# h of batches 6 and 7 in 512-token pieces, their loads in halves, and a new order behind the first operations

## The chip, the cores and the metric

One core of one Trainium2 chip runs the whole program. The metric is the device time of one execution in microseconds (us), the median over runs. The core has five engines that work side by side and wait for each other by semaphores: TensorE (PE in the profile; PEld is its weight load), VectorE (DVE), ScalarE (ACT), GpSimd (POOL) and SyncE (SP). The last two mostly issue DMAs here.

## The reference

Linear attention with a norm, and then a gated feed-forward block, for 8 batches of 576 tokens. The inputs are float32.

```python
kv = einsum('bhsd,bhse->bhde', k, v)          # 8 heads of 64
o = einsum('bhsd,bhde->bhse', q, kv)
o = o / sqrt(mean(o * o, -1) + 1e-6) * g_norm
x = o with heads side by side                  # 576 x 512 for a batch
h = relu(x @ w_in)                             # 576 x 1024
c[s] = w0 * h[s-1] + w1 * h[s] + w2 * h[s+1]   # conv_w, each channel by itself
out = (h * sigmoid(c)) @ w_out                 # 576 x 512
```

## The kernel before, in words

Everything on chip is bfloat16 except sums in PSUM and the rows that go out. The batches are handled in pairs (0,1), (2,3), (4,5), (6,7); h of a pair is one tile of 128 channels x 8 blocks x 1152 tokens. PSUM is cut into 8 banks by hand.

The program is a list of small operations, each a few instructions. A string, `ORDER` (lines 71 to 135), names them in the order in which they are written into the program, and lines 671 to 679 tie the instructions of each engine to exactly this order. Each engine takes its instructions one after the other; between engines only the data, the PSUM banks and the buffers make them wait. A token is a name with arguments, `!A` or `!V` for ACT or DVE where either could do it, and behind `@` the bank or buffer that its tile gets. The operations, with their lines:

- `Lq`, `Lk`, `Lv` (352 to 363): POOL issues the load of q, k or v of a batch. With a second argument 0 or 1 it is half a batch (288 KB as bfloat16), without it the whole (576 KB). q, k and v have two buffers each, so a load waits until the batch that had the buffer has been read. A load also waits for the load eight before it.
- `kv` (386): PE sums k'v of a batch, 72 matmuls of 64x64, or 36 for a half. `kvc` copies it to SBUF.
- `qt` (411) and `qc` (422): PE transposes q by halves, 36 matmuls each; ACT or DVE copies it.
- `ot` (432): PE makes o, 8 matmuls for half a batch. `sq` (446) squares it on ACT, `oc` (451) keeps it.
- `ss` (477), `ln` (489), `sl` (495): the sums of squares of a pair, the reciprocal root on ACT, and on DVE its split into two bfloat16 parts. `sp` (505) spreads it over the channels on PE and `mu` (516) multiplies on DVE, which makes x. A pair's `ss` needs all eight `sq` of its two batches.
- h in either of two ways. `hm` (529) works on one batch: two halves of 288 tokens, so 128x288 matmuls, with two of the four parts of x in one step; `re` (539) is its relu. `ha` (543) works on a pair, flat over its 1152 tokens: 512 of them at a time, four matmuls; `hb` (556) does the last 128 tokens for four channel blocks, 16 matmuls of 128x128. Their relus are `rea` and `reb`. Batches 0, 1, 6 and 7 go by `hm`, pairs (2,3) and (4,5) by `ha` and `hb`.
- the gate: `ta` (580) two taps, `aa` (587) and `ab` (593) their sums, on DVE; `sg` (599) the sigmoid on ACT; `mg` (606) the product with h on DVE, in place.
- `om` (614): PE multiplies h by w_out, four of the eight channel blocks in one step of four 128x512 matmuls, into one bank; `ea` (633) copies the finished bank into a row buffer (four of them), `st` (641) stores it from SP. Blocks 0 and 1, 2 and 3, and so on of a pair share a store.
- `sw` (660): the next store is held back until the named load has landed.
- `fi`, `fq`, `fo`: matmuls of zeros that fill time on PE.

Of the lists at the top, `CONV`, `OMT`, `NORM`, `HALFOUT` and `STORES2` are read by the program; `STORES2` only says which stores go out as two of 256 KB instead of one of 512 (line 648). `HALF` and `PAIRH` are read nowhere: what they name stands in the order.

The core of `ha` and `hm`:

```python
for t in (2 * u, 2 * u + 1):          # hm: b, f, u
    for e in range(2):
        nc.tensor.matmul(ps[:, e, :HS], w_in_sb[:, t, f * P:(f + 1) * P], x[:, t, e * HS:(e + 1) * HS], ...)
...
for t in range(NT):                   # ha: p, f, e
    nc.tensor.matmul(ps, w_in_sb[:, t, f * P:(f + 1) * P], x[:, t, e * 512:(e + 1) * 512], ...)
```

Of the kernel before, what the change touches and what calls it, by code (L numbers as in the profile page):

```python
# [68 lines left out]


# [20 lines left out]
qc.3.0!V@0 oc.3.3@2 aa.1.0 mg.1.3 sq.3.3@4 om.0.1.1.0@2 oc.3.2 ta.1.3@1 om.0.1.0.0 ea.0.1.0!A@1 Lk.5.1@0 Lq.4.1@1
ta.1.2 om.0.1.0.1@6 om.0.0.1.0 ab.1.0 sq.3.2@5 ea.0.0.0!A aa.1.1 ab.1.1 om.0.1.1.1 sg.1.0 qt.5.1@0 qt.5.0@2 kv.3.0@4
qc.5.1!V@1 sg.1.1 ea.0.1.1!V qc.5.0!V@2 kvc.3.0!A Lq.4.0 om.0.2.1.1@7 mg.1.0 sg.1.3 sg.1.2 ot.3.0@0,4 om.0.2.1.0@6
sq.3.1@6 om.0.3.1.1@2 Lv.5.1@0 sq.3.0@7 ss.2@3 ss.3 ln.1@0 mg.1.1 oc.3.1@3 oc.3.0 sl.1@0 om.0.2.0.1 om.0.3.0.1 st.0.0
ea.0.3.1!A@2 kv.5.1@4 qt.4.1@0 Lk.5.0 sp.3.1.1@2 kvc.5.1!V Lk.4.1@1 mu.3.1.1@0 sp.2.0.1@4 mu.2.0.1 om.0.2.0.0
qc.4.1!A@0 sp.3.0.0@0 sp.3.1.0@2 ea.0.2.1!A@0 om.0.3.1.0@7 sp.3.0.1@4 mu.3.0.0 Lv.5.0 sp.2.1.1@0 mu.3.1.0 om.0.3.0.0
mu.3.0.1 sp.2.1.0@2 ea.0.2.0!A sp.2.0.0@4 mu.2.1.1 mu.2.0.0 mu.2.1.0 hb.1.0@6 Lv.4.1@1 fq.1.256.0@0 kv.4.1@0
ea.0.3.0!A kv.5.0@4 reb.1.0!A@1 kvc.5.0!V ot.5.1@6,2 kvc.4.1!A sq.5.2@0 oc.5.2@0 sq.5.3@1 ha.1.3.0@0 rea.1.3.0!V
ha.1.3.1@1 rea.1.3.1!V oc.5.3 ta.2.3@0 Lk.4.0 ot.5.0@6,4 ha.1.2.0@0 Lv.4.0 rea.1.2.0!V ha.1.2.1@3 oc.5.0@1 rea.1.2.1!V
ta.2.2 sq.5.1@2 Lk.7@0 oc.5.1 aa.2.1 ha.1.1.1@1 kv.4.0@4 sq.5.0@3 rea.1.1.1!A ot.4.1@6,2 kvc.4.0!A qt.4.0@0 oc.4.2@2  # L100
sq.4.3@4 qc.4.0!V@0 ab.2.1 oc.4.3 sq.4.2@5 ha.1.1.0@4 rea.1.1.0!A ta.2.1@1 ha.1.0.0@5 rea.1.0.0!A ha.1.0.1@2
ot.4.0@0,3 rea.1.0.1!A ta.2.0 aa.2.0 sq.4.1@6 sq.4.0@7 ha.1.6.0@5 ha.1.5.1@2 ss.4@6 oc.4.1@3 oc.4.0 ss.5 rea.1.5.1!A
ln.2@0 Lq.7@0 qt.7.1@3 qc.7.1!A@0 qt.7.0@0 om.0.4.0@2 sl.2@0 om.0.4.1 ab.2.0 ha.1.5.0@3 Lv.7@0 rea.1.6.0!A sp.5.0.1@4
sp.5.1.1@6 mu.5.0.1@1 qc.7.0!A@1 Lv.6@1 ea.0.4!A@3 sp.4.1.1@0 mu.4.1.1 ha.1.4.0@2 rea.1.5.0!A sg.2.0 hb.1.1@3 Lq.6@1
mu.5.1.1 sp.5.1.0@0 rea.1.4.0!V sp.5.0.0@4 kv.7@6 ha.1.4.1@2 reb.1.1!A kvc.7!A sp.4.0.0@6 mu.5.0.0 mu.5.1.0 sg.2.1
rea.1.4.1!A sp.4.1.0@4 mu.4.0.0 sp.4.0.1@0 mu.4.1.0 ha.1.7.1@3 sg.2.3 mu.4.0.1 sw.q.6 st.0.4 hb.2.1@2 reb.2.1!V@0
sg.2.2 ot.7.0@4,6 mg.2.0 Lk.6@1 ta.2.5@1 rea.1.7.1!A oc.7.1@0 ta.2.4 kv.6@0 ha.1.7.0@2 kvc.6!V sq.7.1@0 ha.2.3.0@3
oc.7.0 ha.2.7.0@6 sq.7.0@1 aa.2.2 ha.1.6.1@7 rea.1.7.0!A ot.7.1@4,0 rea.2.3.0!A rea.1.6.1!V ab.2.2 rea.2.7.0!A
qt.6.0@2 ha.2.7.1@6 oc.7.2@1 sq.7.3@2 sq.7.2@3 oc.7.3 ha.2.6.0@7 mg.2.1 ta.2.6@0 sg.2.4 qc.6.0!V@0 rea.2.7.1!A
ha.2.2.0@4 ha.2.1.0@0 ha.2.4.0@1 rea.2.4.0!V ha.2.3.1@5 sg.2.5 ta.2.7 rea.2.6.0!A rea.2.1.0!A rea.2.2.0!A aa.2.3  # L110
sw.k.6 st.0.3 ab.2.3 rea.2.3.1!A mg.2.2 ha.2.0.0@2 qt.6.1@0 rea.2.0.0!A ot.6.0@6,3 ta.3.7@1 oc.6.0@2 sq.6.0@4
ha.2.6.1@5 oc.6.1 ha.2.5.1@2 ha.2.2.1@6 qc.6.1!A@0 rea.2.6.1!A sw.k.6 st.0.2 sq.6.1@5 sg.2.6 ta.3.6 ha.2.1.1@7 aa.3.3
sg.2.7 mg.2.3 rea.2.1.1!A hb.2.0@0 om.1.2.0.1@1 ha.2.0.1@3 ab.3.3 reb.2.0!A rea.2.2.1!A rea.2.0.1!A om.1.0.0.1@4
ha.2.5.0@5 ta.3.1@0 om.1.2.1.0@0 om.1.2.1.1 rea.2.5.0!A rea.2.5.1!A sg.3.6 ot.6.1@2,5 oc.6.3@3 om.1.2.0.0 ea.1.2.1!A@0
sq.6.2@6 sq.6.3@7 om.1.0.1.1 om.1.4.1@1 om.1.0.1.0@5 sg.3.7 ea.1.0.1!A@2 ss.6@6 ss.7 ta.3.0 aa.3.0 ab.3.0 om.1.3.1.1@4
om.1.0.0.0 mg.3.3 ta.3.3@1 om.1.3.0.1 ln.3@0 sl.3@0 ea.1.0.0!A om.1.3.1.0@7 ea.1.3.1!V@3 ea.1.2.0!A oc.6.2 sp.6.0.1@5
sp.6.1.1@2 om.1.3.0.0 sw.k.6 st.0.1 om.1.4.0 mu.6.0.1@0 ea.1.3.0!A mu.6.1.1 ea.1.4!A@1 sg.3.0 ta.3.2 st.1.2 sp.7.1.0@2
sp.6.0.0@4 sp.7.0.1@6 om.1.1.0.1@0 mu.6.0.0 mu.7.1.0 om.1.1.1.1 om.1.1.0.0@1 mu.7.0.1 aa.3.1 ea.1.1.1!A@0 sp.7.0.0@2
sp.6.1.0@4 sp.7.1.1@6 om.1.1.1.0 mu.6.1.0 mu.7.0.0 ha.2.4.1@0 hm.6.0.0@4 hm.6.0.1 ab.3.1 mu.7.1.1 hm.6.1.0@2 sg.3.1
mg.3.0 ea.1.1.0!A rea.2.4.1!A sg.3.2 hm.6.4.0@0 ta.3.4@0 hm.6.4.1 hm.7.5.0@6 re.6.4!A@1 hm.6.1.1 ta.3.5 aa.3.2  # L120
re.6.1!A hm.7.5.1 re.6.0!A hm.6.6.0@0 hm.6.2.0@2 hm.6.6.1 re.7.5!A hm.6.2.1 hm.7.3.0@4 hm.7.0.0@6 re.6.2!V hm.7.3.1
ab.3.2 re.6.6!A hm.6.5.0@0 sg.3.3 st.1.4 re.7.3!V hm.7.0.1 hm.6.7.0@2 hm.6.7.1 re.6.7!A mg.3.1 hm.7.2.0@4 re.7.0!A
ta.4.7@1 hm.6.5.1 re.6.5!V ta.4.6 aa.4.3 ab.4.3 sg.3.5 sg.3.4 hm.7.7.0@2 hm.7.7.1 hm.7.2.1 mg.3.2 re.7.2!A hm.6.3.0@0
hm.6.3.1 re.6.3!A ta.4.3@0 sg.4.7 ta.4.2 hm.7.1.0@6 hm.7.1.1 hm.7.6.0@4 hm.7.6.1 re.7.6!A st.1.0 hm.7.4.0@0 hm.7.4.1
sg.4.6 aa.4.1 om.2.2.0.0@4 mg.4.3 ab.4.1 re.7.1!A sg.4.2 ta.4.1@1 ta.4.0 aa.4.0 st.1.3 ab.4.0 re.7.4!V sg.4.3 mg.4.1
om.2.1.1.1@5 om.2.0.0.0@6 om.2.2.1.0 ea.2.2.0!A@1 ta.5.6@0 sg.4.1 sg.4.0 om.2.1.0.0@7 re.7.7!A ta.5.7 aa.5.3 mg.4.0
om.2.1.0.1 st.1.1 ta.4.4@1 om.2.3.0.1@4 om.2.3.1.0@0 ab.5.3 om.2.2.1.1@1 sg.5.6 ea.2.1.1!A@0 ta.4.5 om.2.3.1.1
om.2.0.1.0 sg.5.7 om.2.3.0.0 om.2.1.1.0 ea.2.1.0!A st.2.1 aa.4.2 ab.4.2 mg.5.3 om.3.1.0.1@2 om.2.4.1@3 sg.4.4
om.2.0.1.1@5 ta.5.5@0 ta.5.4 om.2.4.0 om.3.0.0.0@7 sg.4.5 aa.5.2 ea.2.3.0!A@2 ea.2.3.1!A mg.4.2 ab.5.2 om.3.1.0.0@0
om.3.0.0.1@4 om.2.0.0.1 ta.5.3@1 om.3.0.1.0 ea.2.4!A@3 ta.5.2 ea.2.0.0!A@0 sg.5.5 aa.5.1 sg.5.4 mg.5.2 ta.5.1@0 st.2.3  # L130
ab.5.1 st.2.4 ta.5.0 aa.5.0 sg.5.2 om.2.2.0.1 om.3.1.1.1 ea.3.0.0!A@2 ea.2.2.1!A ab.5.0 ea.3.1.1!A@3 om.3.5.1@3 st.2.2
om.3.1.1.0 om.3.0.1.1 ea.3.1.0!V sg.5.1 ea.3.0.1!V sg.5.3 mg.5.1 st.3.1 om.3.3.1@2 om.3.4.1@0 sg.5.0 st.3.0 om.3.2.1@1
mg.5.0 ea.2.0.1!V st.2.0 om.3.4.0 ea.3.4!A@1 om.3.2.0 om.3.5.0 ea.3.2!V@3 om.3.3.0 st.3.4 st.3.2 ea.3.5!A@2 st.3.5
ea.3.3!V@0 st.3.3 om.3.6.1@0 ea.3.6.1!V@1 st.3.6.1 om.3.6.0 ea.3.6.0!A@3 st.3.6.0
"""


# [572 lines left out]
```

## Time and profile before

| | us |
|---|---|
| median of 3 runs | 179.40 (179.26 to 179.43) |
| the profiled execution, its own time | 179.12 |
| its span on the core | 177.3 |
| PE busy | 170.3 |
| DVE busy | 157.0 |
| ACT busy | 139.7 |
| POOL busy | 34.7 |

The span is the time from the first to the last instruction; 1.8 us of the execution lie around it. Times inside it count from its start. The granted clock of PE was 0.999 of full. A busy time is the sum of an engine's instruction times, overlaps counted once; matmuls are pipelined, so that a matmul of 379 ns may be followed by the next after 216, and what a step costs is read from start to start. Loads move 15.1 MB into SBUF over the software queue, stores 9.4 MB out.

In the order of the work: the pair (0,1) is prepared up to some 43 us, much of it beside fillers; the h of (2,3) runs to about 93, that of (4,5) to about 126, that of 6 and 7 from 126.5 to 142.5, and `om` of (4,5) and (6,7) fill the rest to 173.7.

### The profile page before, as it was taken

What the parts mean: (1) busy time and instruction counts of PE and PEld (TensorE: products, weight loads), DVE (VectorE), ACT (ScalarE), POOL (GpSimd) and SP (SyncE); (2) the same over time, 40 slices, a digit from 0 to 9 for tenths busy, and PEclk for the clock granted to TensorE, in tenths of its full rate; (3) what the DMA queues carried; (4) which work ended last, traced back from release to release, by engine and by line L of the source; (5) the groups of instructions that cost most, each with busy time, mean ns of one, the idle gap of its engine ahead of it and who ended that gap; (6) DMA issues with size and microseconds to landing.
All of it is one profiled execution on the core that took longest, in us unless ns stands there. A gap on an engine that the chain in (4) does not pass through costs nothing.

```text
span 177.3 us, 5289 instructions
## 1 busy us (share of the span) xinstructions
PE 170.3 (96%) x2253; PEld 95.4 (54%) x2253; DVE 157.0 (89%) x282; ACT 139.7 (79%) x219; POOL 34.7 (20%) x60
## 2 busy tenths in 40 slices
PE   7999998899999999999999999999999999999992
PEld 7755765576444454444554454444577754444451
DVE  2757699999999796999999999999999999999931
ACT  2366799899999938999999999987795966494720
POOL 6945640851067005500000000000000000000000
PEclk9999999999999999999999999999999999999999
DMA  5999999999999996999881000005710000043594
GB/s 184 366 201 200 202 206 210 202 206 208 206 207 233 230 206 88 207 210 205 183 301 64 0 2 4 0 3 213 272 49 0 0 0 4 0 172 123 218 379 173
DMA packets 21355, 27.22 MB, mean 153 GB/s; under 512 B 1224, under 2 KB 15828, under 8 KB 21332
## 3 DMA queue, kind: packets, MB, share of 16 engines
q0 software_dynamic: 15072, 15.09, 51.5%
q1 hardware_dynamic: 6256, 11.80, 18.0%
q8 instruction: 17, 0.28, 0.6%
q14 instruction: 6, 0.05, 0.1%
q10 hardware_dynamic: 4, 0.00, 0.0%
HBM read 32.52 MB, written 9.44 MB: 237 GB/s over the span
## 4 chain that ended last, share of the span: by engine, by line
PE 66%; DVE 14%; DMA 8%; ACT 7%; issue 2%; POOL 1%; ACTq 0%; DVEq 0%
PE banks L628 28%; PE banks L534 13%; PE banks L547 12%; DMA v_sb<-in_v_dram 6%; PE banks L296 3%; PE banks L441 2%; ACT sq L448 2%; PE banks L393 2%; ACT h L238 2%; DVE xT L518 2%; DMA out_dram<-row 2%; PE banks L418 2%; DVE taps L583 2%; DVE taps L596 2%; DVE taps L584 1%
## 5 line engine op out<-in xcount | busy, mean ns | idle before, releaser
L628 PE MATMUL banks<-w_out_sb,h 128*128 128x512 bf16 x280 | 63.7, 379 | 0.2
L603 ACT ACTIVATE taps<-taps,cw 128x576 bf16<-128x576 bf16 (+1 forms) x48 | 43.6, 946 | 9.9 <-DVE taps L596 9.8
L628 PEld LDWEIGHTS <-h 128*128 128x128 bf16 x280 | 26.5, 98 | 31.5 <-issue 1.6
L238 ACT ACTIVATE h<-banks 128x512 bf16<-128x512 f32 (+1 forms) x51 | 29.8, 658 | 5.7 <-PE banks L534 4.2
L534 PE MATMUL banks<-xT,w_in_sb 128*128 128x288 bf16 x256 | 33.5, 286 | 0.4
L547 PE MATMUL banks<-xT,w_in_sb 128*128 128x512 bf16 x128 | 30.1, 379 | 0.2 <-ACT row L232 0.2
L534 PEld LDWEIGHTS <-w_in_sb 128*128 128x128 bf16 x256 | 24.6, 98 | 8.3 <-issue 1.6
L232 ACT ACTIVATE row<-banks 128x512 f32<-128x512 f32 (+1 forms) x29 | 16.8, 601 | 9.6 <-PE banks L628 5.6
L590 DVE TENSOR_TENSOR taps<-taps 128x1152 bf16<-128x1152 bf16 (+1 forms) x24 | 22.9, 956 | 0.5
L596 DVE TENSOR_TENSOR taps<-taps,h 128x1152 bf16<-128x1152 bf16 (+1 forms) x24 | 22.8, 952 | 0.3
L609 DVE TENSOR_TENSOR h<-h,taps 128x1152 bf16<-128x1152 bf16 (+1 forms) x24 | 22.7, 951 | 0.2 <-ACT taps L603 0.2
L583 DVE TENSOR_SCALAR taps<-h,cw 128x576 bf16<-128x576 bf16 (+1 forms) x48 | 20.3, 423 | 1.7 <-ACT h L238 1.5
L448 ACT ACTIVATE sq<-banks 128x576 bf16<-128x576 f32 x32 | 20.4, 674 | 1.7 <-PE banks L441 1.7
L584 DVE TENSOR_SCALAR taps<-h,cw 128x576 bf16<-128x576 bf16 (+1 forms) x48 | 20.1, 418 | 0.0
L547 PEld LDWEIGHTS <-w_in_sb 128*128 128x128 bf16 x128 | 11.8, 98 | 14.4 <-issue 1.3
L518 DVE SCALAR_TENSOR_TENSOR xT<-o,cw,banks 128x576 bf16<-128x576 f32 x24 | 18.1, 806 | 0.4 <-PE banks L511 0.3
L232 ACT ACTIVATE o<-banks 128x576 f32<-128x576 f32 x24 | 15.9, 678 | 0.0
L240 DVE TENSOR_SCALAR h<-banks 128x576 bf16<-128x576 f32 (+1 forms) x17 | 12.2, 720 | 1.1 <-PE banks L547 1.0
L354 POOL DMA_DIRECT2D k_sb<-in_k_dram x12 | 8.7, 726 | 20.0 <-PE banks L441 9.4
...
L354 POOL DMA_DIRECT2D v_sb<-in_v_dram x13 | 9.4, 724 | 11.2 <-PE banks L324 4.7
L354 POOL DMA_DIRECT2D q_sb<-in_q_dram x13 | 9.6, 738 | 7.5 <-PE banks L418 6.5
...
## 6 DMA issues: line engine op xcount, KB each, us to landing
...
```

The source lines that it names most:

```text
L232: nc.scalar.activation(to, fr, AX.Copy)
L238: nc.scalar.activation(to, fr, AX.Relu)
L354: loads[x, b] = nc.gpsimd.dma_start(out=qkv(x, b)[:, w0:w0 + n, :], in_=rows(x, b, w0, n))
L448: nc.scalar.activation(by_r(s), natural(T["ot", b, t][:, :S]), AX.Square)
L534: nc.tensor.matmul(ps[:, e, :HS], w_in_sb[:, t, f * P:(f + 1) * P], x[:, t, e * HS:(e + 1) * HS], start=(t == 0), stop=(t == NT - 1))
L547: nc.tensor.matmul(ps, w_in_sb[:, t, f * P:(f + 1) * P], x[:, t, e * 512:(e + 1) * 512], start=(t == 0), stop=(t == NT - 1))
L583: nc.vector.tensor_scalar_mul(tap[:, 0, f % 2, :n, 8:8 + S], h[:, f], cw[:, f:f + 1])
L590: nc.vector.tensor_add(tap[:, 1, :, :n, :S], tap[:, 0, :, :n, 7:7 + S], tap[:, 1, :, :n, 1:1 + S])
L596: nc.vector.tensor_add(y, y, h[:, 2 * j:2 * j + 2])
L603: nc.scalar.activation(y, y, AX.Sigmoid, scale=scale)
L609: nc.vector.tensor_mul(h, h, T["tap", c, j][:, 1, :, :n, :S])
L628: nc.tensor.matmul(ps[:, 0], h[:, f, m * P:(m + 1) * P], w_out_sb[:, f, :], start=first and f == 4 * i, stop=not first and f == 4 * i + 3)
```

## The change

Tokens 1 to 244 of the order are the same. Behind them:

- h of batches 6 and 7: the 32 `hm` and 16 `re` are replaced by 16 `ha`, 2 `hb` and their 18 relus for the pair (6,7).
- Loads of 6 and 7: six whole loads become twelve halves; `kv` of 6 and 7 becomes four halves with four `kvc`.
- One filler, `fq.1.256.0`, is left out (two matmuls of zeros, ahead of kv of batch 4).
- The order of everything is another, with other banks, buffers and, for some copies and relus, the other engine. The counts of `om`, `st`, `ta`, `aa`, `ab`, `mg`, `sg`, `sp`, `mu` stay.

The program issues 2219 matmuls instead of 2253, and 22 loads of q, k and v instead of 16 behind v of batch 3.

The lists:

```diff
-HALF = [0, 1, 2, 3, 4, 5]
+HALF = [0, 1, 2, 3, 4, 5, 6, 7]
-PAIRH = [1, 2]
+PAIRH = [1, 2, 3]
-STORES2 = [(0, 0), (0, 3), (0, 2), (0, 1)]
+STORES2 = [(0, 2), (0, 0), (0, 3), (0, 1)]
```

The order of the loads behind v of batch 3 (`Lv.3.0`), with the other tokens left out:

```diff
-Lk.5.1@0 Lq.4.1@1 Lq.4.0 Lv.5.1@0 Lk.5.0 Lk.4.1@1 Lv.5.0 Lv.4.1@1 Lk.4.0 Lv.4.0 Lk.7@0 Lq.7@0 Lv.7@0 Lv.6@1 Lq.6@1 Lk.6@1
+Lv.5.0@0 Lk.5.1@0 Lv.5.1 Lk.5.0 Lq.4.0@1 Lk.7.0@1 Lv.7.0@1 Lk.7.1 Lq.4.1 Lk.4.1@0 Lq.7.0@0 Lv.7.1 Lv.4.1@0 Lk.4.0 Lv.4.0 Lv.6.1@0 Lq.6.0@1 Lk.6.0@0 Lq.6.1 Lq.7.1 Lk.6.1 Lv.6.0
```

PE's order from kv of batch 5 to the norm sums of batches 4 and 5:

```diff
-kv.5.1 qt.4.1 sp.3.1.1 sp.2.0.1 om.0.2.0.0 sp.3.0.0 sp.3.1.0 om.0.3.1.0 sp.3.0.1 sp.2.1.1 om.0.3.0.0 sp.2.1.0 sp.2.0.0 hb.1.0 fq.1.256.0 kv.4.1 kv.5.0 ot.5.1 ha.1.3.0 ha.1.3.1 ot.5.0 ha.1.2.0 ha.1.2.1 ha.1.1.1 kv.4.0 ot.4.1 qt.4.0 ha.1.1.0 ha.1.0.0 ha.1.0.1 ot.4.0 ha.1.6.0 ha.1.5.1 ss.4 ss.5
+kv.5.0 kv.5.1 sp.2.0.0 sp.2.1.0 sp.2.1.1 om.0.3.0.1 om.0.3.0.0 sp.2.0.1 sp.3.1.1 sp.3.0.0 om.0.3.1.0 ha.1.3.0 sp.3.0.1 sp.3.1.0 qt.4.1 ha.1.2.0 qt.4.0 ot.5.1 ha.1.2.1 hb.1.0 ha.1.3.1 ha.1.1.0 ot.5.0 kv.4.1 ha.1.0.1 ha.1.0.0 ot.4.1 kv.4.0 ha.1.1.1 om.0.4.1 ot.4.0 om.0.4.0 kv.7.0 ss.4 ss.5
```

Stores: in both orders the first one goes out alone and the others of the pair (0,1) are held back by `sw`.

```diff
-st.0.0 ... sw.q.6 st.0.4 ... sw.k.6 st.0.3 ... sw.k.6 st.0.2 ... sw.k.6 st.0.1
+st.0.2 ... sw.k.6 st.0.0 ... sw.v.6 st.0.3 ... sw.v.6 st.0.4 ... sw.v.6 st.0.1
```

The end of the order (DVE's last gate products, PE's last steps and the last stores):

```diff
-ab.5.0 ea.3.1.1!A om.3.5.1 st.2.2 om.3.1.1.0 om.3.0.1.1 ea.3.1.0!V sg.5.1 ea.3.0.1!V sg.5.3 mg.5.1 st.3.1 om.3.3.1 om.3.4.1 sg.5.0 st.3.0 om.3.2.1 mg.5.0 ea.2.0.1!V st.2.0 om.3.4.0 ea.3.4!A@1 om.3.2.0 om.3.5.0 ea.3.2!V@3 om.3.3.0 st.3.4 st.3.2 ea.3.5!A@2 st.3.5 ea.3.3!V@0 st.3.3 om.3.6.1 ea.3.6.1!V@1 st.3.6.1 om.3.6.0 ea.3.6.0!A@3 st.3.6.0
+mg.5.0 ea.3.0.1!V om.3.3.1 ea.3.1.0!V ea.3.0.0!A st.3.0 om.3.5.1 sg.5.2 sg.5.3 om.3.2.1 om.3.4.1 ea.3.1.1!A st.3.1 mg.5.1 st.2.0 om.3.5.0 ea.3.5!A@2 om.3.4.0 ea.3.4!A@0 st.3.5 om.3.2.0 om.3.3.0 st.3.4 om.3.6.1 ea.3.2!V@3 st.3.2 ea.3.3!V@1 st.3.3 ea.3.6.1!A@2 st.3.6.1 om.3.6.0 ea.3.6.0!A@0 st.3.6.0
```

More of the change, by code (lines that the diff above doesn't have):

```diff
@@ L90 @@
 Lk.3.0 sq.2.2@3 oc.2.2 kvc.3.1!V ot.3.1@0,3 ta.1.0@0 Lv.3.0 ea.0.0.1!A@0 ab.1.3 ta.1.1 qt.3.0@5 sg.1.7 sg.1.6
[L91 to L134, printed above, removed]
+qc.3.0!V@0 oc.3.3@2 aa.1.0 mg.1.3 sq.3.3@4 ab.1.0 ta.1.2@1 om.0.1.1.1@2 sq.3.2@5 om.0.1.1.0@6 oc.3.2 om.0.1.0.0 ta.1.3
@@ new lines @@
+om.0.1.0.1 Lv.5.0@0 aa.1.1 sg.1.1 ab.1.1 om.0.0.1.0 qt.5.0@0 qt.5.1@3 Lk.5.1@0 qc.5.1!V@1 ea.0.1.0!A@1 kv.3.0@5
+ea.0.1.1!A sg.1.0 kvc.3.0!A ea.0.0.0!V sg.1.2 om.0.2.1.0@2 ot.3.0@3,5 Lv.5.1 sg.1.3 qc.5.0!V@2 sq.3.0@6 om.0.2.1.1@7
+om.0.3.1.1@0 sq.3.1@7 ss.2@1 ss.3 ln.1@0 mg.1.0 oc.3.1@3 mg.1.1 om.0.2.0.0 om.0.2.0.1 ea.0.2.0!A@2 oc.3.0 Lk.5.0
+sl.1@0 ea.0.2.1!V kv.5.0@1 kvc.5.0!A kv.5.1@5 sp.2.0.0@3 mu.2.0.0@0 kvc.5.1!A sp.2.1.0@1 sp.2.1.1@5 mu.2.1.0 mu.2.1.1
+om.0.3.0.1 om.0.3.0.0@7 sp.2.0.1@1 sp.3.1.1@3 Lq.4.0@1 mu.2.0.1 sp.3.0.0@5 om.0.3.1.0 mu.3.1.1 Lk.7.0@1 mu.3.0.0
@@ new lines @@
+Lv.7.0@1 ea.0.3.1!A@3 ha.1.3.0@0 Lk.7.1 sp.3.0.1@1 sp.3.1.0@3 ea.0.3.0!A Lq.4.1 qt.4.1@5 rea.1.3.0!A@1 mu.3.0.1
+ha.1.2.0@7 Lk.4.1@0 Lq.7.0@0 qc.4.1!A@0 Lv.7.1 rea.1.2.0!A mu.3.1.0 qt.4.0@0 Lv.4.1@0 Lk.4.0 ot.5.1@2,4 sq.5.2@0
+oc.5.2@0 ha.1.2.1@6 qc.4.0!V@3 rea.1.2.1!V hb.1.0@0 ha.1.3.1@1 oc.5.3 sq.5.3@1 ha.1.1.0@2 rea.1.3.1!A rea.1.1.0!A
+ot.5.0@6,4 oc.5.0@1 sq.5.1@2 reb.1.0!V ta.2.2@0 Lv.4.0 kv.4.1@0 oc.5.1 sq.5.0@3 ha.1.0.1@3 ha.1.0.0@2 ta.2.3 aa.2.1
+kvc.4.1!V rea.1.0.1!V rea.1.0.0!A ab.2.1 ot.4.1@0,4 oc.4.2@2 kv.4.0@6 kvc.4.0!A ha.1.1.1@3 rea.1.1.1!V ta.2.1@1 ta.2.0
@@ new lines @@
+aa.2.0 sq.4.3@4 oc.4.3 om.0.4.1@2 ot.4.0@6,3 sq.4.2@5 sq.4.0@6 sq.4.1@7 om.0.4.0 oc.4.0@3 kv.7.0@0 ss.4@5 ss.5 oc.4.1
+st.0.2 ln.2@0 ha.1.5.1@7 kvc.7.0!A sl.2@0 ha.1.4.1@3 ea.0.4!A@2 rea.1.5.1!A sg.2.2 ha.1.5.0@0 rea.1.4.1!V sp.4.0.1@1
+sp.5.0.0@6 sp.4.1.1@4 ha.1.7.1@3 mu.4.0.1@1 mu.5.0.0 rea.1.7.1!A Lv.6.1@0 mu.4.1.1 ha.1.6.1@1 rea.1.5.0!A rea.1.6.1!A
+ab.2.0 ha.1.4.0@7 rea.1.4.0!A sp.4.0.0@2 sp.5.1.0@0 sp.4.1.0@4 sg.2.3 mu.5.1.0 mu.4.1.0 ha.1.7.0@6 hb.1.1@7 Lq.6.0@1
+Lk.6.0@0 sp.5.1.1@0 sp.5.0.1@4 rea.1.7.0!A ha.1.6.0@6 sg.2.1 reb.1.1!A sg.2.0 mu.4.0.0 qt.7.0@2 Lq.6.1 mu.5.1.1
@@ new lines @@
+mu.5.0.1 rea.1.6.0!A qc.7.0!V@0 Lq.7.1 qt.7.1@0 qc.7.1!V@1 mg.2.1 Lk.6.1 ha.2.6.1@7 rea.2.6.1!A@0 sw.k.6 st.0.0
+ot.7.0@2,4 sq.7.0@0 ta.2.5@0 oc.7.0@0 oc.7.1 kv.7.1@0 ha.2.3.0@6 rea.2.3.0!A ta.2.4 kvc.7.1!V hb.2.0@7 sq.7.1@1
+reb.2.0!A ha.2.5.0@2 qt.6.0@3 rea.2.5.0!A ot.7.1@0,5 aa.2.2 ab.2.2 mg.2.0 oc.7.3@1 ha.2.6.0@7 ha.2.0.0@2 sq.7.3@2
+qc.6.0!V@0 oc.7.2 sq.7.2@3 ha.2.1.1@6 ha.2.4.1@0 rea.2.6.0!A sg.2.5 sg.2.4 ta.2.7@1 rea.2.0.0!A ha.2.2.0@7 ha.2.7.1@1
+ta.2.6 aa.2.3 rea.2.1.1!V rea.2.7.1!A ab.2.3 rea.2.2.0!A Lv.6.0 ha.2.0.1@3 rea.2.0.1!A mg.2.2 ha.2.1.0@2 ha.2.7.0@1
@@ new lines @@
+rea.2.4.1!A rea.2.1.0!A rea.2.7.0!A sw.v.6 st.0.3 kv.6.0@6 kvc.6.0!A kv.6.1@2 qt.6.1@4 ot.6.0@0,6 kvc.6.1!A sg.2.7
+qc.6.1!V@0 sg.2.6 oc.6.0@2 ta.3.1@0 sq.6.0@4 mg.2.3 ta.3.0 om.1.1.0.0@2 sq.6.1@5 om.1.3.0.1@3 oc.6.1 aa.3.0
+om.1.0.0.1@4 om.1.1.0.1@5 hb.2.1@0 ab.3.0 om.1.1.1.1 reb.2.1!A ea.1.1.1!A@0 ot.6.1@6,0 sq.6.2@6 ta.3.7@1 om.1.1.1.0
+sq.6.3@7 sw.v.6 st.0.4 oc.6.3@3 om.1.3.1.1 ea.1.3.1!V@2 ss.6@5 ss.7 ln.3@0 ta.3.6 sl.3@0 aa.3.3 ha.2.2.1@0 om.1.0.1.1
+om.1.3.0.0@1 om.1.3.1.0 oc.6.2 ea.1.1.0!A rea.2.2.1!A ea.1.0.1!A@3 ea.1.3.0!A sg.3.0 sp.7.1.1@6 sp.6.1.1@4 sp.7.0.0@2
@@ new lines @@
+om.1.0.1.0@0 mu.7.0.0@0 sw.v.6 st.0.1 mu.6.1.1 om.1.2.1.0@1 mu.7.1.1 sp.6.1.0@2 sp.7.0.1@4 mu.6.1.0 om.1.0.0.0
+ea.1.0.0!A mu.7.0.1 st.1.3 om.1.2.0.0 ea.1.2.0!A@1 ab.3.3 sp.6.0.1@6 mu.6.0.1 sp.7.1.0@2 sp.6.0.0@4 mu.6.0.0
+om.1.4.1@0 ha.2.3.1@1 om.1.2.0.1@7 sg.3.1 om.1.4.0 ha.2.5.1@4 mu.7.1.0 ha.3.6.0@2 ha.2.4.0@3 mg.3.0 sg.3.7 ha.3.7.0@5
+ha.3.0.0@6 om.1.2.1.1 ta.3.2@0 rea.2.3.1!A ta.3.3 aa.3.1 ab.3.1 sg.3.6 rea.2.4.0!A mg.3.3 ta.3.4@1 ha.3.1.0@1
+rea.3.7.0!A@1 ha.3.2.1@3 ea.1.2.1!A rea.2.5.1!A ha.3.2.0@7 ha.3.3.1@4 ta.3.5 aa.3.2 ea.1.4!A@2 rea.3.2.0!V ha.3.7.1@0
@@ new lines @@
+sg.3.3 ha.3.6.1@5 rea.3.3.1!A rea.3.7.1!V rea.3.2.1!A ha.3.3.0@7 ab.3.2 sg.3.2 mg.3.1 ta.4.2@0 rea.3.6.0!A hb.3.1@0
+ha.3.5.1@2 rea.3.3.0!A st.1.2 ta.4.3 aa.4.1 sg.3.4 sg.3.5 mg.3.2 ha.3.1.1@7 ha.3.4.0@3 ab.4.1 reb.3.1!A ta.5.7@1
+rea.3.1.0!V rea.3.5.1!A st.1.1 om.2.0.0.0@4 ha.3.4.1@0 rea.3.4.0!A sg.4.3 rea.3.6.1!A hb.3.0@3 rea.3.4.1!A ta.5.6
+sg.4.2 aa.5.3 om.2.2.1.1@2 ab.5.3 mg.4.1 rea.3.1.1!A om.2.2.0.1 ha.3.5.0@5 sg.5.7 ta.4.7@0 ta.4.6 om.2.1.0.1@0 sg.5.6
+aa.4.3 st.1.4 mg.5.3 rea.3.0.0!A rea.3.5.0!A ab.4.3 sg.4.7 om.2.0.1.1@1 ta.4.4@1 sg.4.6 ta.4.5 ea.2.2.1!A@0 ha.3.0.1@7
@@ new lines @@
+om.2.0.0.1 rea.3.0.1!A aa.4.2 om.2.1.1.1 st.1.0 ea.2.0.1!A@1 om.2.3.1.1@5 om.2.0.1.0 om.2.2.1.0@6 mg.4.3 ab.4.2
+ta.4.1@0 om.2.3.1.0@2 ta.4.0 om.2.4.1@1 om.2.3.0.0 aa.4.0 ab.4.0 sg.4.5 sg.4.4 mg.4.2 ta.5.5@1 ea.2.3.0!A@2 ta.5.4
+reb.3.0!V om.2.2.0.0 ea.2.2.0!A sg.4.1 sg.4.0 mg.4.0 st.2.2 aa.5.2 ab.5.2 ea.2.0.0!A sg.5.5 ta.5.0@0 ta.5.1
+om.2.1.0.0@2 om.2.1.1.0 om.3.1.1.0@6 om.2.4.0 ea.2.4!A@0 ea.2.1.0!A@3 aa.5.0 sg.5.4 ab.5.0 st.2.4 om.3.0.0.0@7
+om.3.1.0.0 ea.2.1.1!A om.3.0.1.1@4 om.3.0.0.1 mg.5.2 ta.5.2@1 sg.5.0 om.3.1.0.1@3 om.2.3.0.1 om.3.1.1.1 om.3.0.1.0
@@ L135 @@
+ea.2.3.1!A ta.5.3 aa.5.1 ab.5.1 st.2.1 sg.5.1 st.2.3 mg.5.0 ea.3.0.1!V@0 om.3.3.1@0 ea.3.1.0!V@3 ea.3.0.0!A st.3.0
+om.3.5.1@1 sg.5.2 sg.5.3 om.3.2.1@2 om.3.4.1@4 ea.3.1.1!A st.3.1 mg.5.1 st.2.0 om.3.5.0 ea.3.5!A@2 om.3.4.0 ea.3.4!A@0
+st.3.5 om.3.2.0 om.3.3.0 st.3.4 om.3.6.1@3 ea.3.2!V@3 st.3.2 ea.3.3!V@1 st.3.3 ea.3.6.1!A@2 st.3.6.1 om.3.6.0
+ea.3.6.0!A@0 st.3.6.0
 """
```

## Prediction

> **What bounds the kernel now.** The first view is the page's table of busy time: TensorE (PE) is busy 96% of the span. A busy share can hide waiting, so I read the stages next: time in us, then the busy time of PE, PEld, DVE, ACT and POOL, the granted clock, the DMA share and GB/s.
>
> ```profile
> PE 170.3 (96%) x2253; PEld 95.4 (54%) x2253; DVE 157.0 (89%) x282; ACT 139.7 (79%) x219; POOL 34.7 (20%) x60
> ...
> 50.00:56.00 6.00, 5.89 (x136) 2.99 (x135) 5.96 (x12) 6.00 (x12) 3.20 (x6) 1.00 1.21 206
> 56.00:60.00 4.00, 4.00 (x74) 1.80 (x76) 2.72 (x6) 3.78 (x7) 1.90 (x3) 1.00 1.16 262
> 60.00:64.00 4.00, 3.92 (x75) 1.74 (x60) 3.73 (x7) 2.44 (x4) 0.00 (x0) 1.00 1.22 211
> 72.00:86.00 14.00, 13.78 (x313) 7.48 (x313) 13.59 (x21) 13.77 (x23) 2.22 (x3) 1.00 1.21 208
> ```
>
> The reader is to see two things. PE has no gap worth naming at full clock, so PE work sets the time. And the DMA engines are full with the q, k and v loads at 206 to 208 GB/s. Only in 56 to 60 is it more, because an output store runs beside them.
>
> The chain of waits shows where the two meet (start us, us, what):
>
> ```profile
> 53.53 0.41 PE banks L393 x36
> 53.95 0.29 issue
> 54.24 0.72 POOL k_sb L354
> 54.95 0.08 issue
> 55.03 0.71 POOL v_sb L354
> 55.74 10.40 DMA v_sb<-in_v_dram
> 66.14 0.04 issue
> 66.19 0.82 PE banks L393 x72
> ```
>
> PE's kv of batch 4 starts at 66.19, 0.05 us after its v has landed. A filler stands just ahead of it (PE timeline, `fq` at 65.80, two matmuls of zeros, to 66.19). So here the load sets the time and PE is just covered. Everywhere else behind 48 us the matmuls follow each other at their own rate.
>
> The end, from DVE's timeline:
>
> ```profile
> 166.83 1.43 DVE L609 TENSOR_TENSOR h<-h,taps 128x1152 bf16<-128x1152 bf16 x2
> 168.17 0.68 DVE L234 COPY row<-banks 128x512 f32<-128x512 f32 x1
> ```
>
> The last gate product ends at 168.25 and the matmul that reads it starts at 168.49. DVE is 0.24 us ahead: a second limit right behind PE.
>
> **The change, part by part.** Which parts act: `HALF` and `PAIRH` are read by nothing, and `STORES2` only for membership. All comes from the order string. Its first 244 tokens are equal, up to 50.5 us; before that nothing moves.
>
> *h of batches 6 and 7.* Out go 32 `hm` steps of four 128x288 matmuls. One step takes 0.49 us (start to start, L534): 15.7 us. In come 16 `ha` of four 128x512 matmuls at 0.863 (L547: 20 matmuls in 4.3 us) and 2 `hb` of 16 at 0.9 to 1.0 (L562): 13.8 + 1.8 = 15.6 us. That is -0.1 us, since the columns streamed are the same. Relu, net of what the order moves between the two engines in other batches: out 12 on ACT at 0.53 and 4 on DVE at 0.67, in 16 on ACT at 0.48 and 2 on DVE at 0.60; three 128x1152 qT copies go from ACT (1.01 each) to DVE (0.67 each). Net ACT -0.8, DVE -0.4 us: both inside engines that PE covers.
>
> *kv of 6 and 7 in halves:* 2 x 0.71 becomes 4 x 0.35 us. Nothing. *The filler:* -0.39 us of PE. Excursions from full matmuls to 64- or 32-row ones and back cost 0.1 to 0.2 us each; there are 23 in both orders: nothing.
>
> So PE alone would end 0.46 us sooner: -0.39 - 0.07.
>
> *The loads.* Six more issues on POOL at 0.72 us: 4.3 us, on an engine that is 20% busy and idle behind 75. Hidden. What counts is their order. Behind v of batch 3 (issued 38.58, landed 13.5 later, 52.08) the old order has nine loads of 288 KB and then the last v of batch 4 as tenth, which landed 11.7 us after its issue at 57.16, at 68.84. The new order is v5, k5, v5, k5, q4, **k7, v7, k7**, q4, k4, **q7, v7**, v4, k4, v4: the last v of batch 4 is the **fifteenth**. It puts batch 7 into the buffers that kv of batch 3 frees at 54, and batch 4 into those that kv of batch 5 frees at 60.3. At 206 GB/s a load of 288 KB takes 1.43 us. The queue stays full (batch 4's loads issue from 60.4 to 64, when transfers are still some two loads behind), so the fifteenth lands at 68.84 + 5 x 1.43 = **76.0**, and the thirteenth, v for the first kv of batch 4, at 73.1.
>
> When does PE get there? The old order reaches its second kv of batch 4 at 72.09. The new one has the same 13 `om` and one `hb` ahead of it, 7 `ha` instead of 5 (+1.73), one more `qt` (+0.31) and `ot` (+0.27), no filler (-0.39): 74.0. The first kv of batch 4 comes at 71.65. So PE waits 73.1 - 71.65 = 1.5 us and then to 76.0, together 2.0 us.
>
> Bounds on this wait, which the trace of before does not show. Above: 2.2, if the landing lags a little more. Below: the old 16.76 us for ten loads are 14.3 of transfer, some 1.46 lost to the early store (in 56 to 60 the engines moved 4 x 262 = 1048 KB, the store is 524 of them, the loads would have had 824) and 1.0 unexplained. The new order also sends one store of 512 KB early, st.0.2, data ready at 59.4 and 60.8, so it falls into the same queue; if it costs nothing and the rest doesn't recur, the load lands at 73.6: no wait. I take 1.6, near the row of before, with half of the unexplained part dropped.
>
> Who stands behind: PE takes its instructions in order, so every later `ha` and `om` moves. DVE and ACT get no relief, since the norm of batches 4 and 5 (`ss`, `ln`, `sl`) hangs on the same kv. What was covered by PE's fill is gone, and nothing later has slack to give it back: behind `ss` of batch 5 both orders have 94.9 us of PE work.
>
> [...] Row first: halves moved at 206 GB/s (50 to 56), whole loads of 576 KB at 208 (72 to 86). [...]
>
> *DVE.* By the last gate product the new order has 0.7 us more DVE work done than the old one (two evacuations fewer are left behind it: -1.2 + 0.4 elsewhere). DVE had 0.24. Its idle time of 3.6 us from 50 to 82 (waits for `ss`, `sp`, `ha`) may shrink or not. Between -0.2 and +0.9; I take 0.1, as the wait for v delays PE and DVE alike and the order puts an evacuation under each gate.
>
> *The tail.* Old: last `om` ends at 173.7, the last evacuation starts at 174.28, 0.4 late by a row buffer whose store had not landed. New: three stores of 512 KB are released 6.5, 5.4 and 4.9 us ahead of PE's end, in the old order 7.7, 6.9 and 4.8 (SP's issues at 166.0, 166.8, 168.9); the last evacuation needs the row of st.3.4, queued behind them. 0 to +0.6; I take 0.2.
>
> Sum: -0.46 + 1.6 + 0.1 + 0.2 = +1.4 us. The profiled execution took 179.12 (span 177.3 and 1.8 around it), 0.28 under the median 179.40. So 180.5 there, and on the median's scale 180.8; I round to **180.7**.
>
> **The rivals.**
> 1. *The loads are in time* (0.25). For it: st.0.2 may slip between loads, and the old order's lag need not recur. Against: the rate of 206 GB/s is flat over 16 us. Then only -0.46 and the tail: 178.9 to 179.4. Faster, the other side.
> 2. *DVE becomes the bound* (0.10). The gate products come 0.5 to 0.9 us late, the loads cost under 0.5: 179.4 to 180.2. It decides once DVE's last product ends later than 5.2 us ahead of PE's end. For it: 0.24 us of lead. Against: ACT and DVE work fall in sum.
> 3. *Both, or a wait that I have not followed* (0.10): a bank or a row held up by a store. Three stores of batches 0 and 1 wait for batch 6's last load, which lands near 90 now; first use near 107. 182 to 183.5.
> 4. *The forecast* (0.55): 179.8 to 181.6.
>
> Halves that cost time as such (a fixed price per load) are in 3: kv of batch 6 comes at 103 and its last load near 90, 13 us of cover.
>
> Measurement tells about 0.2% (0.36 us) from no change. Faster by more: most of rival 1, 0.22. Same: the rest of 1 and part of 2, 0.13. Slower: 0.65. The range reaches from rival 1 to the lower edge of rival 3: 178.8 to 182.2.
>
> **What would show it.** Right: in the chain a "DMA v_sb" piece of 11 us or more that ends near 76, PE idle of over 1 us between 71 and 76 (its busy time in the windows under 9), and every PE step behind it moved by the same amount. L534 has 128 matmuls left, L547 192, L562 96. Wrong: PE runs through 71 to 76 without a gap; or the idle time stands at the gate products (PE L628 waiting for DVE L609) behind 105 us; or the last store group grows by more than 0.6 us.

## The result, and the profile after

The changed kernel takes 181.57 us (median of 5 runs, 181.23 to 182.78), against 179.43 (5 runs, 179.26 to 179.62) for the kernel before: 1.0127 times as long, 95% interval 1.0105 to 1.0150. It is slower by about 2.1 us. Its profiled execution took 181.23 us with a span of 179.5; before it was 179.12 and 177.3, so the spans differ by 2.2 us.

All line numbers of the kernel after are higher by one than those of before: `ha` is L548, `kv` L394. The experiments have the numbers of before.

The page's busy line of the kernel after:

```profile
PE 170.0 (95%) x2219; PEld 90.4 (50%) x2219; DVE 156.6 (87%) x281; ACT 139.8 (78%) x224; POOL 38.8 (22%) x66
```

PE's busy time is 0.3 us less than before, and the kernel is 2 us slower: the time went into waiting. The stages of the kernel after show where (time, then busy time of PE, PEld, DVE, ACT, POOL, the granted clock, the DMA share, GB/s):

```profile
50.00:56.00 6.00, 6.00 (x138) 2.99 (x137) 5.93 (x12) 5.94 (x12) 1.62 (x3) 1.00 1.21 206
56.00:60.00 4.00, 4.00 (x81) 1.82 (x82) 2.58 (x6) 3.97 (x7) 1.24 (x2) 1.00 1.21 207
60.00:64.00 4.00, 3.87 (x68) 1.74 (x54) 3.96 (x7) 1.23 (x4) 3.29 (x5) 1.00 1.19 231
64.00:67.00 3.00, 1.55 (x11) 0.49 (x8) 2.85 (x4) 1.19 (x2) 1.02 (x2) 1.00 1.17 252
71.00:74.00 3.00, 3.00 (x56) 1.34 (x54) 2.75 (x6) 2.28 (x5) 0.00 (x0) 1.00 1.09 187
72.00:86.00 14.00, 13.22 (x198) 6.01 (x197) 13.37 (x22) 13.08 (x24) 5.02 (x7) 1.00 0.80 125
```

Most of the loss is in 64 to 67, where half of PE's time is lost while the DMA engines move the most of these stages (252 GB/s: loads and one store side by side). In 71 to 74, where the prediction had put the loss, PE is full. Smaller losses, 0.78 us in sum, follow in 72 to 86.

Every idle time of PE behind 50 us, as PE's timeline of the kernel after marks them (start, busy time, work, and in brackets the idle time ahead of it and what ended it):

```profile
67.05 0.48 PE L419 MATMUL banks<-ident,q_sb 64*64 64x64 bf16 x36 [1.50 <-DMA q_sb<-in_q_dram]
...
76.05 0.48 PE L394 MATMUL banks<-v_sb,k_sb 64*64 64x64 bf16 x36 [0.21 <-DMA v_sb<-in_v_dram]
...
83.83 0.42 PE L512 MATMUL banks<-wparts,spread 32*128 32x288 bf16 x6 [0.39 <-DVE wparts L503]
84.43 2.75 PE L548 MATMUL banks<-xT,w_in_sb 128*128 128x512 bf16 x12 [0.18 <-DVE h L241]
...
91.50 1.04 PE L548 MATMUL banks<-xT,w_in_sb 128*128 128x512 bf16 x4 [0.16 <-DVE xT L519]
```

Two waits for loads, 1.50 + 0.21 = 1.71 us, and three for DVE, 0.73 us. Before, the same view marks one, 0.16 us, for a copy on ACT:

```profile
82.77 1.02 PE L547 MATMUL banks<-xT,w_in_sb 128*128 128x512 bf16 x4 [0.16 <-ACT row L232]
```

The first wait of the kernel after is that of `qt.4.1`, for the second half of q of batch 4, the ninth load of the list.

The chain of waits passes through the load queue once more, and then through DVE:

```profile
64.27 11.64 DMA v_sb<-in_v_dram
75.91 0.14 issue
76.05 0.48 PE banks L394 x36
...
83.26 0.52 DVE wparts L503
83.77 0.60 DVE h L241
84.38 2.17 DVE xT L519 x3
86.55 1.27 DVE taps L597
87.82 3.63 DVE xT L519 x5
91.50 1.04 PE banks L548 x4
```

The last v of batch 4 is now on the chain until 75.91; before, the chain left the queue at 66.14, with the other half of that v. Behind 91.5 the chain is PE's until the last evacuation. The end, from the timelines of PE, DVE and ACT:

```profile
169.19 0.75 DVE L610 TENSOR_TENSOR h<-h,taps 128x1152 bf16<-128x1152 bf16 x1
...
173.74 1.91 PE L622 MATMUL banks<-w_out_sb,h 128*128 128x256 bf16 x16
...
175.10 0.38 ACT L233 ACTIVATE row<-banks 128x256 f32<-128x256 f32 x1 [2.24 <-DMA out_dram<-row]
175.76 0.38 ACT L233 ACTIVATE row<-banks 128x256 f32<-128x256 f32 x1 [0.28 <-PE banks L622]
```

PE's last step before, from its timeline:

```profile
171.95 1.91 PE L621 MATMUL banks<-w_out_sb,h 128*128 128x256 bf16 x16
```

The last step starts at 173.74 instead of 171.95: 1.79 later. From there to the end of the span it is 5.76 us, before 5.35: the tail is 0.41 longer. The last gate product ends at 169.94, and no step of PE waits for it. The bracket of the second-last evacuation names a row buffer whose store had not landed.

So the 2.2 us are: 1.71 of waits for loads, 0.57 more of other waits of PE (0.73 for DVE, less the 0.16 of before), 0.41 of tail, and what is left, 0.49 less, which is put down to less work of PE (0.46 was forecast). That last part is a remainder of two single traces and good to some tenths: PE's transposes of batch 5, up to which the two orders give PE the same work, start at 52.86 instead of 52.73.

### The profile page after: what moved, and what is told of

Read it like the earlier page. It is cut to its first block, busy times and chain, and to the rows that moved or that the text cites. A ratio compares the mean times of both kernels' runs of the same rounds, so it can differ in the third digit from the quotient of the medians.

```text
span 179.5 us, 5229 instructions
## 1 busy us (share of the span) xinstructions
PE 170.0 (95%) x2219; PEld 90.4 (50%) x2219; DVE 156.6 (87%) x281; ACT 139.8 (78%) x224; POOL 38.8 (22%) x66
## 4 chain that ended last, share of the span: by engine, by line
PE 61%; DVE 19%; DMA 10%; ACT 3%; POOL 2%; issue 2%; SPq 0%; ACTq 0%; DVEq 0%
PE banks L629 30%; PE banks L548 16%; DMA v_sb<-in_v_dram 6%; DMA stg<-in_v_dram 4%; DVE xT L519 3%; PE banks L535 3%; DVE taps L585 3%; DVE h L241 3%; PE banks L394 2%; DVE taps L591 2%; DVE taps L584 2%; PE banks L563 2%; DVE taps L597 2%; PE banks L442 2%; ACT sq L449 1%
## 5 line engine op out<-in xcount | busy, mean ns | idle before, releaser
L629 PE MATMUL banks<-w_out_sb,h 128*128 128x512 bf16 x280 | 64.6, 379 | 0.1
L548 PE MATMUL banks<-xT,w_in_sb 128*128 128x512 bf16 x192 | 45.3, 380 | 0.3 <-DVE h L241 0.2
L239 ACT ACTIVATE h<-banks 128x512 bf16<-128x512 f32 (+1 forms) x55 | 31.3, 616 | 7.7 <-PE banks L548 3.6
L548 PEld LDWEIGHTS <-w_in_sb 128*128 128x128 bf16 x192 | 17.8, 98 | 21.4 <-issue 1.8
L233 ACT ACTIVATE row<-banks 128x512 f32<-128x512 f32 (+1 forms) x30 | 17.3, 585 | 10.6 <-PE banks L629 5.3
L535 PE MATMUL banks<-xT,w_in_sb 128*128 128x288 bf16 x128 | 17.3, 286 | 0.4
L355 POOL DMA_DIRECT2D v_sb<-in_v_dram x15 | 10.8, 725 | 24.2 <-PE banks L394 14.6
L535 PEld LDWEIGHTS <-w_in_sb 128*128 128x128 bf16 x128 | 12.2, 97 | 4.5 <-issue 1.3
L235 DVE COPY qT<-banks 128x1152 bf16<-128x1152 bf16 x14 | 10.4, 750 | 4.6 <-PE banks L419 4.6
L355 POOL DMA_DIRECT2D k_sb<-in_k_dram x14 | 10.1, 720 | 13.5 <-PE banks L394 8.6
L355 POOL DMA_DIRECT2D q_sb<-in_q_dram x15 | 10.8, 722 | 3.8 <-PE banks L419 3.0
```

The source lines that it names most:

```text
L233: nc.scalar.activation(to, fr, AX.Copy)
L239: nc.scalar.activation(to, fr, AX.Relu)
L355: loads[x, b] = nc.gpsimd.dma_start(out=qkv(x, b)[:, w0:w0 + n, :], in_=rows(x, b, w0, n))
L629: nc.tensor.matmul(ps[:, 0], h[:, f, m * P:(m + 1) * P], w_out_sb[:, f, :], start=first and f == 4 * i, stop=not first and f == 4 * i + 3)
```

## The experiments

Each is an edit of the order string of the kernel after, unless another base is named. Ratios are to the kernel before, measured on the same chip, with 95% intervals.

### The second half of q of batch 4 early

The load that PE waited for first is issued right behind the first half. If the waits add up, 1.5 us are won; if the queue as a whole is late, PE only meets the next load.

```diff
-Lq.4.0@1 ... Lk.7.0@1 Lv.7.0@1 Lk.7.1 Lq.4.1
+Lq.4.0@1 Lq.4.1 ... Lk.7.0@1 Lv.7.0@1 Lk.7.1
```

> The changed kernel with one load moved: the second half of q of batch 4 is issued right behind its first half, ahead of the three loads of batch 7 that stood before it. In the changed kernel PE waited 1.6 us for it (67.0). Theory, the full queue: the q lands near 61 and that wait goes, but v of batch 4 is still the thirteenth and fifteenth load and lands at 73.0 and 75.9, so PE now waits there instead (1.4 us at 71.6, 0.4 at 75.6): 181.3 to 181.7, no gain worth naming against 181.57. Rival, one late load: the wait for q is the whole cost, the rest is covered: 180.0.

181.47 us, ratio 1.0116 [1.0060, 1.0173]: nothing won that can be told. PE's timeline of this kernel:

```profile
71.23 0.44 PE L441 MATMUL banks<-qT,kvw 64*64 64x64 bf16 x8
73.29 0.48 PE L393 MATMUL banks<-v_sb,k_sb 64*64 64x64 bf16 x36 [1.62 <-DMA v_sb<-in_v_dram]
```

The wait of 1.50 at 67 is gone, and one of 1.62 stands at the first kv of batch 4, whose v landed at 73.14 as in the kernel after (73.01). That is where the prediction had expected it. The loss belongs to the queue and not to one load.

### The loads of batch 4 ahead of those of batch 7

The five loads of batch 4 that were behind batch 7 take the places of batch 7's, which go behind them. Batch 4 then uses the buffers that kv of batch 3 frees.

```diff
-Lk.7.0@1 Lv.7.0@1 Lk.7.1 Lq.4.1 ... Lk.4.1@0 Lq.7.0@0 Lv.7.1 ... Lv.4.1@0 Lk.4.0 ... Lv.4.0 ... Lv.6.1@0 ... Lk.6.0@0
+Lq.4.1 Lk.4.1@1 Lv.4.1@1 Lk.4.0 Lv.4.0 ... Lk.7.0@0 Lv.7.0@0 Lk.7.1 Lq.7.0@0 Lv.7.1 ... Lv.6.1@1 ... Lk.6.0@1
```

> The changed kernel with the loads of batch 4 ahead of those of batch 7, in the buffers that kv of batch 3 frees; batch 7 takes those that kv of batch 5 frees, batch 6 those of batch 4. All else as changed. Theory, the full queue: the last v of batch 4 is the tenth load again and lands near 69, PE meets no wait for a load before 80, and 1.9 us of PE time come back: 179.4 to 179.9, with what DVE and the tail cost left. Rival, the order of the engines: DVE's late products (the split of the norm and the last mu of batch 5) cost most of it and the loads are beside the point: 180.8 to 181.6.

179.18 us, ratio 1.0001 [0.9973, 1.0029]. Within the interval of some 0.5 us the loss is gone; the median lies 0.2 under the range of the theory, which had left in the cost of DVE and of the tail. The stages in which the kernels above waited, in this one:

```profile
64.00:67.00 3.00, 2.95 (x81) 1.39 (x84) 2.84 (x4) 2.30 (x4) 0.14 (x1) 1.00 1.17 252
...
71.00:74.00 3.00, 2.81 (x65) 1.51 (x69) 2.97 (x6) 2.86 (x6) 0.00 (x0) 1.00 1.13 193
```

The queue is as full as before (252 GB/s in 64 to 67), yet PE is busy: the last v of batch 4 landed at 69.02 instead of 75.90. Nothing about the h pieces or the halves was touched; the buffers of batches 4, 6 and 7 were, which the next experiment leaves alone.

### Three of batch 7's loads ahead, two moved behind

This asks how much of batch 7 may go first. Two loads of batch 7 less in the way of v (q and the last v of batch 7 go behind, and `Lq.4.1` goes early) should be enough by the sum of the prediction, since the thirteenth load lands at 73.1 and PE comes for it at 74.0.

```diff
-Lq.4.0@1 ... Lk.7.0@1 Lv.7.0@1 Lk.7.1 Lq.4.1 Lk.4.1@0 Lq.7.0@0 Lv.7.1 Lv.4.1@0 Lk.4.0 Lv.4.0
+Lq.4.0@1 Lq.4.1 ... Lk.7.0@1 Lv.7.0@1 Lk.7.1 Lk.4.1@0 Lv.4.1@0 Lk.4.0 Lv.4.0 Lq.7.0@0 Lv.7.1
```

> The changed kernel with three loads moved and no buffer changed: q's second half of batch 4 goes behind its first, and q and v of batch 7 (a half each) go behind v of batch 4, so that only three loads of batch 7 are ahead and the last v of batch 4 is the thirteenth load. Theory, with the point from which it decides: PE comes to it at 74.0, three loads ahead of it cost 3 x 1.43 = 4.3 us of queue and land it near 73.1, so PE doesn't wait, and the time is that of the kernel with all of batch 4 first: 179.0 to 179.6. Rival: any load of batch 7 ahead costs its share, so three of five leave half of the loss: 180.2 to 180.6.

179.34 us, ratio 1.0006 [0.9987, 1.0025]. The last v of batch 4, now thirteenth, landed at 73.13, and PE waited for no load. Its waits for DVE at 81.9 to 89.5 are still there (0.36, 0.18 and 0.17 us). So the load term is worth the difference between 1.0127 and 1.0006, about 2.2 us with some 0.5 on either side (the waits marked in the trace of the kernel after are 1.71; the other terms of the sum above, 0.5 together, should then have been left, which these intervals do not tell). It appears between three and five loads of batch 7 ahead: with five ahead and `Lq.4.1` early as here, the first experiment, it is there.

### The early store held back

The store of 512 KB that runs beside the loads is put behind them.

```diff
-oc.4.1 st.0.2
+oc.4.1 sw.v.4 st.0.2
```

> The changed kernel with one store held: the early store of 512 KB (blocks 4 and 5 of the first pair) waits until the last v of batch 4 has landed, by the same means as the other held stores. Theory: the store took about 1.5 us of the load queue's rate, so the last v lands at 74.4 instead of 75.9, the second half of q near 65.3 instead of 67.0, and the time falls by 1.4 to 1.6 us: 180.0 to 180.2. Rival: the store runs in spare bandwidth, the loads land as before: 181.4 to 181.7; or the store, now late, holds up the row buffer that the evacuation of block 8 needs near 80: over 181.6.

180.11 us, ratio 1.0037 [1.0015, 1.0059]. Against the kernel after that is 0.0090 of 179.4, or 1.6 us won, with some 0.6 on either side. The landing times that the theory named can't be read from its trace: that execution ran at half clock for 3.4 us near 11, and the transposes of batch 5 start at 54.55 in it instead of 52.86. What the store takes from the loads shows in the pair of kernels with batch 4 first (below): with the store held, the last v of batch 4 landed at 67.49 instead of 68.82, 1.33 us earlier.

### The halves alone, on the kernel before

The six whole loads of batches 6 and 7 become two halves each, in place; all else is the kernel before.

```diff
-Lk.7@0 ... Lq.7@0 ... Lv.7@0 ... Lv.6@1 ... Lq.6@1 ... Lk.6@1
+Lk.7.0@0 Lk.7.1 ... Lq.7.0@0 Lq.7.1 ... Lv.7.0@0 Lv.7.1 ... Lv.6.0@1 Lv.6.1 ... Lq.6.0@1 Lq.6.1 ... Lk.6.0@1 Lk.6.1
```

> The kernel before with one part of the change alone: each of the six whole loads of batches 6 and 7 becomes two halves, issued one behind the other in the same places; all else as before. Theory, the full queue moves halves as fast as whole loads: the last load lands within 1 us of where it did, and nothing waits for it: 179.2 to 179.6, no change. [...]

179.45 us, ratio 1.0011 [0.9996, 1.0026]: no difference. The last load landed at 89.26 instead of 88.68. With eight loads in flight, six more issues moved the last landing by 0.58 us, 0.1 us each at most, and cost the kernel nothing that can be told.

### A store of the tail moved ahead

`st.2.0` stood behind two stores of the last pair's rows; here it goes out ahead of `st.2.3`.

```diff
-st.2.3 ... mg.5.1 st.2.0
+st.2.0 st.2.3 ... mg.5.1
```

> The changed kernel with one store moved on SP: the store of blocks 0 and 1 of the third pair, whose data are ready near 160, goes two places ahead of where it was among the last ones. Theory of the tail: the last stores are queued behind three of 512 KB, and 0.3 to 0.7 us come back at the end: 180.9 to 181.3. Rival: the end is set by the last store's own landing: 181.5, no change.

180.86 us, ratio 1.0085 [1.0058, 1.0112], 0.0042 less than the kernel after: 0.75 us won, with some 0.6 on either side. The traces say it more closely: from the start of PE's last step to the end of the span it is 5.04 us instead of 5.76, and the same 5.04 instead of 5.74 where the move is made with batch 4 first (below). So 0.7 us are won in the tail, more than the 0.41 that the change had added there: the tail is then shorter than the 5.35 of the kernel before.

### Both, and the store held as well

The second and the sixth edit together, and then the store held back on top.

> The changed kernel with batch 4's loads first and the store of blocks 0 and 1 of the third pair moved ahead: the two gains side by side. Theory: they are at different places of the one chain and add up, 179.2 - 0.6 = 178.4 to 178.8, faster than both kernels. Rival: the tail is set by the last products, which come just as late: 179.0 to 179.3.

> As the one before, and the early store of the first pair also waits until the last v of batch 4 has landed. Theory: with batch 4 first no PE step waits for a load any more, so 1.5 us earlier landings are covered anyway: the same as the one before within 0.2 us. Rival: a late hold pushes other stores, or a load wait is left that it removes: off by over 0.4 us, either way.

178.36 us, ratio 0.9943 [0.9922, 0.9964], and 178.40, ratio 0.9940 [0.9922, 0.9959]. The first of them beats both kernels, as its theory said. The store held back, worth 1.6 us where the loads were late, is worth nothing once they are in time. PE's idle times that are left in the first of them are three waits for DVE, 0.16, 0.18 and 0.16 us.

### DVE's lateness and POOL's issues

In the kernel after two of the first taps of the pair (2,3) took 0.79 us instead of 0.52, and POOL issued seven loads in a row from 76.85 to 81.87. Behind these taps on DVE stands the split of the norm of batches 4 and 5, for which PE waits. DVE's timeline and POOL's:

```profile
78.27 0.72 POOL L355 DMA_DIRECT2D k_sb<-in_k_dram  x1
...
78.76 0.52 DVE L585 TENSOR_SCALAR taps<-h,cw 128x1152 bf16<-128x1152 bf16 x1
...
78.99 1.44 POOL L355 DMA_DIRECT2D q_sb<-in_q_dram  x2
...
79.20 0.79 DVE L584 TENSOR_SCALAR taps<-h,cw 128x1152 bf16<-128x1152 bf16 x1
79.92 0.80 DVE L585 TENSOR_SCALAR taps<-h,cw 128x1152 bf16<-128x1152 bf16 x1
```

Three of the seven are moved up, in the kernel after and in the best one.

```diff
-Lv.4.0 ... Lv.6.1@0 ... Lq.6.0@1 Lk.6.0@0 ... Lq.6.1 ... Lq.7.1 Lk.6.1
+Lv.4.0 Lq.6.0@1 Lq.6.1 Lq.7.1 ... Lv.6.1@0 ... Lk.6.0@0 ... Lk.6.1
```

> The kernel after with three of the seven loads that POOL issues back to back (both halves of q of batch 6 and the last one of batch 7) moved up to stand right behind the last v of batch 4, so that POOL no longer issues them beside the first two tap multiplications of DVE at 79 to 81 us. Theory (POOL's issuing slows those two instructions from 0.51 to 0.79 us, and DVE's lateness there, worth 0.3 to 0.5 us at the step of h that waits, comes from it): the two take about 0.51 us again, the wait at that step shrinks by 0.3 to 0.5, and the time is 181.0 to 181.3 us. Rival (DVE is late there for its order alone, and the slow instructions have slack): 181.5 us, the wait as it was.

> The same move on the kernel that has the loads of batch 4 first and the stores of the last pair spread (178.4 us). Theory: the step of h that waits 0.3 us for DVE waits less, 178.0 to 178.2 us. Rival: no change, 178.4 us.

181.06 us, ratio 1.0117 [1.0077, 1.0157], and 178.22, ratio 0.9938 [0.9923, 0.9952]. In both the taps took 0.51 to 0.52 (in the best kernel they had done so already; there the cast that begins the split had been slow, 0.57 us, and now took 0.31). PE's waits for DVE shrank, from 0.73 to 0.16 and from 0.50 to 0.16. (In the first one the view also names DVE for 1.61 us at `qt.4.1`. That is counted with the loads: the q landed at 67.29 and the step started at 67.33.) In the times nothing of it can be told: 0.001 and 0.0005 less than without the move, inside the intervals, though both medians come out at or near the range of the theory. In the first one part of the wait came back elsewhere: the last v of batch 4 landed 0.44 later, and PE's waits for loads are 1.96 us instead of 1.71. So the local effect is shown, and its worth, at most 0.34 us in the second kernel by PE's idle time, is not resolved.

The theory's words fail in one point: in the first one POOL still issued loads beside the four taps (the last two of the row of four, from 78.71 to 80.29), and the taps were not slow. What changed is the phase, which the last section takes up.

## Why the prediction was right, and where it was not

It said slower, 180.7 us; it is slower, 181.57. The mechanism that it named, the queue of loads that puts batch 7 ahead of batch 4, is the cause: moving loads alone, with no buffer changed, brings the time back to that of before (the third experiment), and freeing the queue of a store wins most of it (the fourth). By its steps:

- **The work of PE**, -0.46 us. `ha` and `hb` went at 0.863 and 0.89 us from start to start. By the idle times above PE's last step should be 2.28 later without that term, and it is 1.79 later: 0.49, good to some tenths. The working beside it has a slip that does not enter the sum: the relus and copies that it lists make -1.7 us on ACT and +0.5 on DVE, not -0.8 and -0.4. The busy times moved by +0.1 and -0.4.
- **The landing times.** The fifteenth load was put at 76.0 and landed at 75.90, the thirteenth at 73.1 and landed at 73.01. The rate of 206 GB/s with a full queue held, and so did the 2.4 us that the old order had lost beside it: from the landing of batch 3's v at 52.04 the fifteen loads took 23.87 us, of which 15 x 1.43 = 21.5 are transfer. The part of it that the prediction called unexplained, 1.0, is not the store's: with batch 4 first and the store held, ten loads still took 15.43 us for 14.3 of transfer. What it is stays open.
- **Where PE waits.** This step failed in its place. Under "When does PE get there?" only the two kv were compared with their loads, and q of batch 4 was left out. The prediction's own numbers put its landing six places of 1.43 us ahead of the fifteenth, at 67.4 (it landed at 66.99); in the trace PE is free for it at 65.55. The sum did not suffer, since the three deficits (q, first kv, second kv) are not added: whoever waits first delays PE for the others. The first experiment shows the same wait at the place that was forecast.
- **The size of the wait**, 1.6 forecast, 1.71 measured, and near in part by luck. The working gave 2.0, and 0.4 came off for loads that would land sooner. They did not: the load landed at 75.90. Instead PE came later: without the 1.71 of waits it would have reached the second kv at 76.05 - 1.71 = 74.34, not at 74.0.
- **The early store**, put at 1.46 us by its share of the bytes. Held back, 1.6 us are won with some 0.6 on either side, and the landing moves by 1.33.
- **Halves cost nothing**: the sum has no term for them, and 1.0011 [0.9996, 1.0026] was measured. The rows of before, 206 GB/s with halves and 208 with whole loads, were right: with six more loads the last one came 0.58 us later.
- **DVE**, 0.1 forecast, 0.57 measured (less the one wait for ACT of before), and at another place: not at the gate products, as the second rival had it, but behind the norm of batches 4 and 5, at 83.8 to 91.5, where PE waits for the split, a relu and the product that makes x. The reason given, that the wait for v delays PE and DVE alike, is not enough: without any wait for loads the three waits stand at 0.71 (the third experiment). In the last two experiments, where POOL issues three loads elsewhere, only 0.16 is left. The term was inside its bounds and its value too small.
- **The tail**, 0.2 forecast, 0.41 measured, inside the bounds. The stores that are released close together are the reason: one of them moved ahead took 0.7 off the tail.

The difference of 0.87 us between forecast and median is thus mostly DVE (0.47) and the tail (0.21), then the loads (0.11) and the rounding from 180.8 to 180.7. The first rival, loads in time, would have taken 178.9 to 179.4: that is the kernel with batch 4 first, 179.18. What it lacked was only the order of five loads.

Of the signs that were named, the chain's piece of over 11 us that ends near 76 is there (11.64, to 75.91). PE's idle time of over 1 us between 71 and 76 is not, and PE's running through that stretch without a gap was named as a sign against; by these alone one would have dropped a right cause.
